# Transposes on 64x128 tiles, shorter runs for q and k, and a new order of steps in a fused attention and wave-MLP kernel

## The chip, the cores and the metric

The kernel runs on one core of a Trainium2 chip. The metric is the device time of one execution in microseconds; runs are compared by the median of several.

## What is computed

q, k and v have the shape (8, 8, 576, 64): batch, heads, positions, head dimension. Attention is local: each chunk of 64 positions sees only itself. Its output is rearranged to x of shape (8, 576, 512) and goes through a phase block with four weights.

```python
scores = (1 / sqrt(64)) * q_c @ k_c.T          # per batch, head and chunk of 64
attn = softmax(scores)
x = (attn @ v_c)                               # -> (8, 576, 512)
theta = x @ w_theta
zr, zi = x * cos(theta), x * sin(theta)
y = einsum('ts,bsd->btd', w_tok_r, zr) + einsum('ts,bsd->btd', w_tok_i, zi)
u = x + y
out = u + maximum(u @ w_ch, 0)
```

Inputs and output are float32; on the chip the matmuls work on float16.

## The kernel before

Four pairs of batches are worked through. A pair has 9 tiles of 128 rows, in five groups: A and B are two tiles each of the pair's first batch, C and D two tiles each of its second, M is the one tile in the middle that holds the last 64 positions of both. A step is one small stage of one group or tile, and its name in the table ORDER says which: `T.0M.1` is stage T of pair 0, group M, in PSUM slot 1.

The stages of a group: loads `q`, `k`, `v`; `T` transposes q and k on PE (`qk_t`), `tq` and `tk` copy the result out of PSUM; `S` the scores, `e` their exps; `V0`, `V1` attention times v for four heads each, `v0`, `v1` divide by the sums; `X` transposes x, `x` copies it; `H` is theta, `g` cosine and sine, `z` the products zr and zi. For group M the products of one half of the rows must change partitions, so `z` sends a tile `zmid` over SP's queue. Then tile by tile: `Y` (nine matmuls against the transposed token weights, for which all z of the batch and M must be there), `y` adds x, `U` and `u` transpose the sum, `W` multiplies by w_ch, `w` is the last addition and the store on SP's queue. Once per run: `lw.00` and `lw.01` load the token weights, `cw` casts the first, `TW` transposes them in three parts and `twd`, `twa` copy these out; `lt` and `lc` load the other two weights.

The steps of all engines are emitted in the order of the table, and each engine works through its own part of it strictly in that order. There are three two-bank PSUM slots (`wide`) for all stages up to H, and two one-bank slots (`thin`) for Y, U and W. q, k, v and most weights are loaded by POOL's queue, which casts them to float16; a load waits until its buffer is free (`nat`, eight of them for q and k; v has room for two pairs). Every 64x64 transpose is its own matmul with its own weight load, addressed to one quarter of the PE array. q and k lie in a tile with two successive positions per partition, so that a DMA reads 512 bytes in one piece.

Of the kernel before, what the change touches and what calls it, by code (L numbers as in the profile page):

```python
# [18 lines left out]
lw.00 q.0M init.00 cw.00 q.0B q.0A TW.00.0 v.0M k.0M q.0C k.0A new.00 T.0M.1 new.10  # L19
tq.0M k.0B tk.0M v.0A twd.00 S.0M.2 k.0C T.0A.1 twa.00 lt.00 e.0M V0.0M.0 q.0D T.0B.2  # L20
v.0B tq.0A tk.0A S.0A.1 tk.0B tq.0B V1.0M.2 v0.0M v.0C e.0A S.0B.0 V1.0A.1 v1.0M k.0D
v1.0A T.0C.2 V0.0A.1 e.0B tq.0C lw.01 tk.0C X.0M.0 q.1A S.0C.2 v0.0A q.1B x.0M X.0A.0
e.0C q.1M v.0D x.0A H.0M.1 H.0A.2 V1.0B.0 g.0M k.1A v1.0B g.0A V0.0B.1 v0.0B V0.0C.0
v0.0C k.1B V1.0C.1 k.1M v1.0C X.0B.2 T.0D.0 x.0B z.0A q.1C tq.0D tk.0D X.0C.1 x.0C z.0M
H.0B.2 q.2M S.0D.0 lc.00 g.0B v.1M TW.01.1 v.1A twd.01 q.1D TW.02.2 twa.01 twa.02 e.0D
H.0C.1 g.0C q.2B z.0B twd.02 Y.00.0 y.00 Y.02.1 U.00.0 V1.0D.2 T.1A.0 v1.0D u.00 tq.1A
V0.0D.1 tk.1A Y.01.0 v.1B v0.0D X.0D.2 T.1M.0 x.0D k.1D k.2B y.02 T.1B.1 y.01 tq.1M
U.02.1 U.01.0 k.1C k.2M z.0C tk.1B v.1D H.0D.2 u.02 tk.1M u.01 S.1A.0 W.01.1 w.01 g.0D
e.1A tq.1B W.02.0 Y.03.1 S.1B.2 V0.1A.1 S.1M.0 w.02 z.0D v0.1A e.1B q.2A e.1M Y.04.0
V1.1M.1 V0.1M.2 y.03 q.3A V1.1A.0 y.04 Y.06.1 v1.1A v1.1M v0.1M T.1D.0 y.06 tq.1D  # L30
# [6 lines left out]
x.1C w.04 e.2M tk.2B u.07 H.1C.2 tq.2B W.07.0 z.1D W.05.1 w.07 q.3D Y.11.0 v.2M w.05
U.10.1 new.20 V1.2M.0 g.1C u.10 S.2A.1 V0.2M.2 y.11 W.08.0 v.3C Y.12.1 e.2A z.1C k.2D
v0.2M w.08 v1.2M T.2C.2 S.2B.1 e.2B V1.2A.0 v1.2A v.2D Y.15.0 v.2C tk.2C V0.2A.0 tq.2C
y.12 y.15 T.2D.1 v.3A tq.2D v0.2A V1.2B.2 v1.2B Y.14.1 V0.2B.0 tk.2D X.2M.1 y.14 X.2A.2  # L40
U.15.0 x.2M Y.16.1 S.2D.1 x.2A v0.2B X.2B.0 k.3B y.16 S.2C.2 e.2C U.11.1 u.15 W.10.0
u.11 Y.18.1 w.10 x.2B e.2D y.18 H.2M.2 W.11.0 w.11 U.12.1 H.2A.0 g.2M z.2M V0.2D.1
V1.2C.2 U.18.0 u.12 W.15.1 u.18 w.15 W.12.0 v.3M w.12 v1.2C g.2A k.3C Y.17.1 V1.2D.0
k.3A v0.2D y.17 v1.2D T.3A.2 V0.2C.1 k.3M U.16.0 W.18.1 w.18 H.2B.0 u.16 tk.3A v0.2C
Y.13.0 g.2B U.17.1 tq.3A X.2C.1 y.13 u.17 v.3D T.3M.2 X.2D.0 x.2C U.14.0 W.16.1 u.14
tq.3M x.2D z.2A U.13.0 u.13 w.16 tk.3M H.2C.1 H.2D.0 g.2C W.13.0 W.14.1 T.3B.2 S.3M.1
g.2D z.2B w.13 S.3A.0 w.14 tq.3B tk.3B e.3M Y.20.0 Y.21.1 new.30 z.2C k.3D y.20 W.17.0
e.3A z.2D T.3D.2 V1.3A.1 w.17 tq.3D tk.3D v1.3A v.3B V1.3M.0 Y.24.0 T.3C.2 S.3B.1 v1.3M
tk.3C y.21 V0.3A.0 y.24 U.20.1 u.20 tq.3C Y.23.0 v0.3A X.3A.2 e.3B V0.3M.0 y.23 S.3C.1
U.21.1 e.3C W.20.0 u.21 Y.22.1 w.20 v0.3M x.3A y.22 U.24.0 H.3A.1 U.23.1 u.24 u.23  # L50
W.21.0 g.3A Y.28.1 V0.3C.2 V1.3B.0 w.21 v0.3C V0.3B.1 y.28 Y.27.0 W.23.1 v0.3B V1.3C.2
v1.3B y.27 S.3D.1 w.23 X.3M.0 x.3M e.3D v1.3C Y.25.0 y.25 U.27.1 u.27 H.3M.0 W.24.0 w.24
V1.3D.2 g.3M V0.3D.1 v1.3D W.27.1 v0.3D Y.26.0 w.27 z.3M U.22.1 y.26 X.3C.2 u.22 X.3D.0
X.3B.1 W.22.1 w.22 U.28.0 x.3B x.3D u.28 H.3B.1 U.25.1 z.3A u.25 W.28.0 W.25.1 g.3B
# [9 lines left out]
def kernel(  # L64
# [11 lines left out]
    nc = tc.nc  # L76
    B, H, S, D = q.shape
# [33 lines left out]
    nat = ctx.enter_context(tc.tile_pool(name="nat", bufs=8))  # L111
    tmp = ctx.enter_context(tc.tile_pool(name="tmp", bufs=3))
    pairp = ctx.enter_context(tc.tile_pool(name="pairp", bufs=2))
# [16 lines left out]
    wraw = pairp.tile([P, KT, S], FP32, name="wraw", tag="zi16")  # L130
# [16 lines left out]
    def load_qk(p, g, which):  # L147
        j0, bb, s0 = GROUPS[g]
        if (p, g) not in nats:
            nats[p, g] = nat.tile([P, 2, H, 2, D], FP16, name="qk16")  # L150
        t = nats[p, g][:, which]
        ap = (q, k)[which]
        if bb is None:
            for b in range(2):
                nc.gpsimd.dma_start(
                    t[half[b], :, 0, :],
                    ap[2 * p + b, :, s0 : s0 + CH, :].rearrange("h s d -> s h d"),
                )
            return
        nc.gpsimd.dma_start(  # L160
            t.rearrange("p h s d -> p h (s d)"),
            ap[2 * p + bb, :, s0 : s0 + GT, :].rearrange(
                "h (p s) d -> p h (s d)", s=2
            ),
        )

    nats = {}

    def load_v(p, g):
        j0, bb, s0 = GROUPS[g]  # L170
        slot = (p % 2) * NT + j0
        if bb is None:
            for b in range(2):
                nc.gpsimd.dma_start(
                    v16[half[b], slot, :, 0:D],
                    v[2 * p + b, :, s0 : s0 + CH, :].rearrange("h s d -> s h d"),
                )
            return
        for r in range(2):
            t0 = s0 + r * P  # L180
            nc.gpsimd.dma_start(  # L181
                v16[:, slot + r, :, 0:D],
                v[2 * p + bb, :, t0 : t0 + P, :].rearrange("h s d -> s h d"),
            )
# [19 lines left out]
    def tok_w(k3, slot):  # L204
        ps = psum2("ps_wT", slot, FP16)
        psv = ps.rearrange("p (r x) -> p r x", r=2)[:, :, 0 : 3 * (KT + 1) * CH]
        psv = psv.rearrange("p r (k t c) -> p r k t c", k=3, c=CH)
        for k in range(3):
            kt = 3 * k3 + k
            for tb in range(KT + 1):  # L210
                for r in range(2 if tb < KT else 1):
                    for h in range(2):
                        if kt < 2 * KT:
                            ri, jl = kt // KT, kt % KT
                            s0 = (jl // 2) * GT + (jl % 2) * CH + h * P
                        else:
                            ri, s0 = h, KT * P
                        nc.tensor.transpose(
                            psv[half[h], r, k, tb, :],
                            wnat[half[r], tb, ri, s0 : s0 + CH],  # L220
                            id16[half[r], half[r]],
                        )
        st["wT", k3] = psv

    def tok_w_copy(k3, r):
        psv = st["wT", k3]
        ks = slice(3 * k3, 3 * k3 + 3)
# [342 lines left out]
```

## Time and profile before

| | |
|---|---|
| median of 3 runs | 237.83 us (234.85 to 238.71) |
| the profiled execution | 235.57 us, its span 233.8 us |
| PE busy | 189.8 us, 81% of the span, 3834 matmuls |
| DVE, ACT, POOL busy | 125.9, 124.2, 76.3 us |
| DMA packets | 87939, of which 80608 under 512 bytes |

The span is what the trace covers; the time contains a little more around it. "Issue" in the chain of waits is time in which an engine waited for nothing that the profile shows. PEclk is the TensorE clock that was granted, as a share of 2.4 GHz. Bytes and packet sizes are those written, so a float32 run of 256 bytes in memory counts as 128.

### The profile page before, as it was taken

The numbers are of one execution on the slowest core, as the hardware profiler recorded it, in microseconds if no ns is written. First come the engines' busy times: TensorE is split into PE (matmuls) and PEld (weight loads), VectorE is DVE, ScalarE is ACT, GpSimd is POOL, SyncE is SP. The second block draws the span as 40 slices with busy tenths as digits, with TensorE's granted clock in tenths as the row PEclk, the third lists the DMA queues.
The fourth block names the chain that finished last, engine by engine and source line by source line (L and its number), as shares of the span: only waits on it lengthen the run. The fifth ranks groups of instructions, "written<-read, shape, count | busy, mean of one in ns | idle before, by whom it ended". The sixth has DMA issues, their size and how long they took to land.

```text
span 233.8 us, 8436 instructions
## 1 busy us (share of the span) xinstructions
PE 189.8 (81%) x3834; PEld 101.5 (43%) x3834; DVE 125.9 (54%) x248; ACT 124.2 (53%) x137; POOL 76.3 (33%) x98
## 2 busy tenths in 40 slices
PE   0252347959799899897949999999999999989971
PEld 0141323535445545453525445555554554444430
DVE  0032402843758784637554476878638784664351
ACT  2434266588572859987612946784763688020210
POOL 8895758877240651599600000000000000000000
PEclk9999999799999999999988999999999999999996
DMA  6999999999996799899991254232022354205444
GB/s 213 173 173 191 174 186 170 182 180 173 142 156 122 89 191 136 67 130 183 219 189 11 48 116 88 47 86 56 6 57 46 81 113 95 45 11 123 89 93 90
DMA packets 87939, 27.70 MB, mean 118 GB/s; under 512 B 80608, under 2 KB 82720, under 8 KB 87904
## 3 DMA queue, kind: packets, MB, share of 16 engines
q0 software_dynamic: 80896, 15.87, 80.2%
q1 hardware_dynamic: 7008, 11.29, 19.5%
q8 instruction: 30, 0.49, 0.9%
q14 instruction: 5, 0.04, 0.0%
HBM read 33.06 MB, written 9.44 MB: 182 GB/s over the span
## 4 chain that ended last, share of the span: by engine, by line
PE 70%; DVE 9%; issue 8%; DMA 6%; ACT 4%; POOL 1%; DVEq 0%; ACTq 0%; POOLq 0%
PE ps_y L441 30%; PE ps_theta L380 14%; PE ps_uw L477 11%; PE ps_qkT L249 4%; PE ps_uT L459 4%; DMA qk<-in_q_dram 3%; DMA qk<-in_k_dram 3%; PE ps_sT L289 3%; DVE u L450 2%; ACT kT L267 2%; DVE x L335 2%; PE ps_x L322 2%; PE ps_xT L355 2%; DVE qT L265 1%; DVE o L486 1%
## 5 line engine op out<-in xcount | busy, mean ns | idle before, releaser
L441 PEld LDWEIGHTS <-wT 128*128 128x128 f16 (+1 forms) x360 | 31.7, 103 | 38.2 <-issue 4.6
L441 PE MATMUL ps_y<-zi,wT 128*128 128x512 f16 (+1 forms) x180 | 45.4, 391 | 0.1
L441 PE MATMUL ps_y<-zr,wT 128*128 128x512 f16 (+1 forms) x180 | 42.3, 391 | 1.7 <-DVE o L486 1.7
L380 PE MATMUL ps_theta<-wtheta,xT 128*128 128x512 f16 x144 | 37.9, 411 | 1.7 <-ACT wT L234 1.2
L450 DVE TENSOR_TENSOR u<-ps_y,x 128x512 f16<-128x512 f32 x36 | 24.5, 688 | 25.0 <-PE ps_y L441 24.9
L477 PE MATMUL ps_uw<-wch,uT 128*128 128x512 f16 x144 | 35.9, 380 | 0.7 <-ACT uT L471 0.7
L486 DVE SCALAR_TENSOR_TENSOR o<-ps_uw,u 128x512 f32<-128x512 f32 x36 | 24.7, 688 | 20.6 <-PE ps_uw L477 20.6
L181 POOL DMA_DIRECT2D v<-in_v_dram x32 | 28.3, 903 | 8.1 <-PE ps_x L322 2.8
L471 ACT COPY uT<-ps_uT 128x512 f16<-128x512 f16 x20 | 11.8, 588 | 36.1 <-PE ps_uT L459 36.1
L265 DVE COPY qT<-ps_qkT 128x1024 f16<-128x1024 f16 (+1 forms) x20 | 12.7, 635 | 32.6 <-PE ps_qkT L249 20.3
L267 ACT COPY kT<-ps_qkT 128x1024 f16<-128x1024 f16 x16 | 16.2, 1015 | 25.0 <-DVE qT L265 20.8
L367 ACT COPY xT<-ps_xT 128x1024 f16<-128x1024 f16 (+1 forms) x20 | 18.3, 930 | 16.7 <-PE ps_xT L355 16.7
L335 DVE TENSOR_TENSOR x<-ps_x,recip 128x512 f16<-128x512 f32 (+1 forms) x40 | 25.5, 638 | 1.4
L249 PE MATMUL ps_qkT<-id,qk 64*64 64x64 f16 x1152 | 16.1, 203 | 11.8 <-issue 8.8
L396 ACT ACTIVATE cos<-ps_theta,pihalf 128x1024 f16<-128x1024 f32 (+1 forms) x20 | 20.6, 1030 | 6.9 <-PE ps_theta L380 6.7
L160 POOL DMA_DIRECT2D qk<-in_q_dram x16 | 14.2, 888 | 25.2 <-PE ps_x L322 9.5
L380 PEld LDWEIGHTS <-xT 128*128 128x128 f16 x144 | 14.3, 104 | 18.2 <-issue 5.3
L249 PEld LDWEIGHTS <-qk 64*64 64x64 f16 x1152 | 13.4, 114 | 14.9 <-issue 11.3
L302 ACT ACTIVATE eT<-ps_sT 128x1024 f16<-128x1024 f32 x16 | 16.4, 1026 | 6.5 <-PE ps_sT L289 6.4
L477 PEld LDWEIGHTS <-uT 128*128 128x128 f16 x144 | 12.9, 98 | 14.3 <-ACT uT L471 1.2
L400 ACT ACTIVATE sin<-ps_theta 128x1024 f16<-128x1024 f32 (+1 forms) x20 | 18.7, 935 | 0.0
L334 DVE RECIPROCAL recip<-ps_x 128x8 f32<-128x8 f32 (+1 forms) x40 | 7.8, 195 | 15.5 <-PE ps_x L322 15.0
(44 smaller groups left out, 184.1 us busy)
## 6 DMA issues: line engine op xcount, KB each, us to landing
out_dram<-o SPq DMA_DIRECT2D x72, 128.0 KB, 2.4
qk<-in_q_dram POOLq DMA_DIRECT2D x16, 256.0 KB, 6.8
qk<-in_k_dram POOLq DMA_DIRECT2D x16, 256.0 KB, 7.5
v<-in_v_dram POOLq DMA_DIRECT2D x32, 128.0 KB, 7.1
wraw<-in_moe_w_tok_r_dram SPq DMA_DIRECT2D x1, 1152.0 KB, 6.2
wnat<-in_moe_w_tok_i_dram POOLq DMA_DIRECT2D x1, 576.0 KB, 12.3
qk<-in_q_dram POOLq DMA_DIRECT2D x8, 64.0 KB, 7.0
v<-in_v_dram POOLq DMA_DIRECT2D x8, 64.0 KB, 6.5
```

The costliest lines, as they stand in the source:

```text
L181: nc.gpsimd.dma_start(v16[:, slot + r, :, 0:D], v[2 * p + bb, :, t0 : t0 + P, :].rearrange("h s d -> s h d"),)
L249: nc.tensor.transpose(psv[half[h], r, e, w, s, :], t[half[r], w, 2 * e + h, s, :], id16[half[r], half[r]],)
L267: nc.scalar.copy(out=t.rearrange("p x c t -> p x (c t)"), in_=ps.rearrange("p x s i -> p x i s"),)
L335: nc.vector.tensor_tensor(out=st[p]["x"][:, j0 : j0 + n, f * NE * D : (f + 1) * NE * D].rearrange("p c (h d) -> p c h d", h=NE), in0=psv[: ...
L367: nc.scalar.copy(out=xT[:, 0 : n * NDB].rearrange("p a (r c) -> p r a c", r=2), in_=psv)
L380: nc.tensor.matmul(ps[:, j * DM : j * DM + DM], xT[:, j * NDB + db, :], wtheta16[:, db, :], start=(db == 0), stop=(db == NDB - 1),)
L396: nc.scalar.activation(out=cos[:, 0:n].rearrange("p a e -> p (a e)"), in_=pin, func=AF.Sin, bias=pihalf, scale=1.0,)
L400: nc.scalar.activation(out=sin[:, 0:n].rearrange("p a e -> p (a e)"), in_=pin, func=AF.Sin)
L441: nc.tensor.matmul(ps[rows], wT[:, kt, cols], z[:, jz, :], start=(i == 0), stop=(i == 2 * KT),)
L450: nc.vector.tensor_tensor(out=u, in0=st[p].pop(("ps_y", j)), in1=st[p]["x"][:, j], op=ALU.add)
L477: nc.tensor.matmul(ps, uT[:, db * P : db * P + P], wch16[:, db, :], start=(db == 0), stop=(db == NDB - 1),)
L486: nc.vector.scalar_tensor_tensor(out=o, in0=st[p].pop(("ps_uw", j)), scalar=0.0, in1=u, op0=ALU.max, op1=ALU.add)
```

## The change

Transposes of q and k, of x and of the token weights use 128 columns of the array instead of 64, so that one instruction does what two did. q and k lie in their tile as v does, one position per partition and tile, with two heads next to each other; a group is loaded by two DMAs of 256-byte runs. The copies, scores and exps follow the new layout. `nat` has seven buffers, and `wraw` one of its own. The table ORDER is another one, with `lw.00` in it a second time near the end. Three of its lines, of 41 before and 41 after, and the core of the code:

```diff
-lw.00 q.0M init.00 cw.00 q.0B q.0A TW.00.0 v.0M k.0M q.0C k.0A new.00 T.0M.1 new.10
+lw.00 init.00 cw.00 q.0B TW.00.0 q.0A q.0M k.0B k.0A twd.00 T.0B.1 tk.0B lt.00 twa.00
...
+v0.3D lw.00 H.3A.1 u.20 w.23 g.3B U.21.0 u.21 g.3A W.20.1 w.20 Y.28.0 z.3B y.28 U.24.1
...
-    nat = ctx.enter_context(tc.tile_pool(name="nat", bufs=8))
+    nat = ctx.enter_context(tc.tile_pool(name="nat", bufs=7))
...
     def load_qk(p, g, which):
-        j0, bb, s0 = GROUPS[g]
         if (p, g) not in nats:
-            nats[p, g] = nat.tile([P, 2, H, 2, D], FP16, name="qk16")
-        t = nats[p, g][:, which]
-        ap = (q, k)[which]
...
-        nc.gpsimd.dma_start(
-            t.rearrange("p h s d -> p h (s d)"),
-            ap[2 * p + bb, :, s0 : s0 + GT, :].rearrange(
-                "h (p s) d -> p h (s d)", s=2
-            ),
-        )
-
-    nats = {}
+            nats[p, g] = nat.tile([P, 2, 2, H, D], FP16, name="qk16")
+        for rows, r, b, t0, n in parts(p, g):
+            nc.gpsimd.dma_start(
+                nats[p, g][rows, which, r],
+                (q, k)[which][b, :, t0 : t0 + n, :].rearrange("h s d -> s h d"),
+            )
...
     def qk_t(p, g, slot):
...
         for w in range(2):
             for e in range(NE):
-                for s in range(n):
+                for j in range(n):
                     for r in range(2):
-                        for h in range(2):
-                            nc.tensor.transpose(
-                                psv[half[h], r, e, w, s, :],
-                                t[half[r], w, 2 * e + h, s, :],
-                                id16[half[r], half[r]],
-                            )
...
+                        nc.tensor.transpose(
+                            psv[:, r, w, e, j, :],
+                            t[half[r], w, j, 2 * e : 2 * e + 2, :].rearrange(
+                                "s h d -> s (h d)"
+                            ),
+                            id16[half[r], half[r]],
+                        )
...
                 for r in range(2):
-                    for h in range(2):
-                        d0 = db * P + h * CH
-                        nc.tensor.transpose(
-                            psv[half[h], r, j * NDB + db, :],
-                            st[p]["x"][half[r], j0 + j, d0 : d0 + CH],
-                            id16[half[r], half[r]],
-                        )
+                    nc.tensor.transpose(
+                        psv[:, r, j * NDB + db, :],
+                        st[p]["x"][half[r], j0 + j, db * P : db * P + P],
+                        id16[half[r], half[r]],
+                    )
```

`parts` gives the two pieces of a group: two tiles of 128 rows of one batch, or for M 64 rows of each batch. The token weights' transposes change likewise: both halves of 64 rows go in one instruction.

Where the table moves instructions, at three places. POOL's queue at the start of the program, before and after (`qk_92`, `qk_103`, `qk_105` are pair 0's groups M, B, A before; `qk_100`, `qk_134`, `qk_137` its B, A, M after; `qk_166` is C before):

```order
L155 DMA qk_92<-in_q_dram 64x8x64 x2
masks.py:197 MEMSET id_79 128x128
masks.py:199 ISA
masks.py:199 AFFINE_SELECT id_79<-id_79 128x128
L160 DMA qk_103<-in_q_dram 128x8x128
L160 DMA qk_105<-in_q_dram 128x8x128
L174 DMA v_87<-in_v_dram 64x8x64 x2
L155 DMA qk_92<-in_k_dram 64x8x64 x2
L160 DMA qk_166<-in_q_dram 128x8x128
L160 DMA qk_105<-in_k_dram 128x8x128
L160 DMA qk_103<-in_k_dram 128x8x128
L181 DMA v_87<-in_v_dram 128x8x64 x2
```

```order
masks.py:197 MEMSET id_79 128x128
masks.py:199 ISA
masks.py:199 AFFINE_SELECT id_79<-id_79 128x128
L160 DMA qk_100<-in_q_dram 128x8x64 x2
L160 DMA qk_134<-in_q_dram 128x8x64 x2
L160 DMA qk_137<-in_q_dram 64x8x64 x2
L160 DMA qk_100<-in_k_dram 128x8x64 x2
L160 DMA qk_134<-in_k_dram 128x8x64 x2
L188 DMA wtheta_81<-in_moe_w_theta_dram 128x4x512
L160 DMA qk_137<-in_k_dram 64x8x64 x2
L168 DMA v_87<-in_v_dram 128x8x64 x2
L168 DMA v_87<-in_v_dram 64x8x64 x2
```

M's loads stand behind those of B and A, C's have left the start, and each load of 128 rows of q or k is now two.

ACT's queue from its first copies to the first cosine, before and after:

```order
L234 COPY wT<-ps_wT 128x3x2x128
L298 ACTIVATE eT<-ps_sT 128x2x256
L267 COPY kT<-ps_qkT 128x1024 x2
L302 ACTIVATE eT<-ps_sT 128x1024 x2
L267 COPY kT<-ps_qkT 128x1024
L367 COPY xT<-ps_xT 128x2x4x64
L302 ACTIVATE eT<-ps_sT 128x1024
L367 COPY xT<-ps_xT 128x2x8x64
L396 ACT_TABLE_LOAD
L396 ACTIVATE cos_718<-ps_theta,pihalf 128x512
```

```order
L263 COPY kT<-ps_qkT 128x1024
L227 COPY wT<-ps_wT 128x3x256
L263 COPY kT<-ps_qkT 128x1024
L289 ACTIVATE eT<-ps_sT 128x1024 x2
L289 ACTIVATE eT<-ps_sT 128x2x256
L352 COPY xT<-ps_xT 128x2x4x64
L352 COPY xT<-ps_xT 128x2x8x64
L381 ACT_TABLE_LOAD
L381 ACTIVATE cos_508<-ps_theta,pihalf 128x512
```

The third k copy and the third full exp, both of group C, no longer stand ahead of the first cosine.

PE around the first Y, before and after; the first `ps_y` is PE's instruction 1,694 before and 942 after, of 7,670 and 5,798 in all:

```order
L380 LDWEIGHTS xT
L380 MATMUL ps_theta<-wtheta_81,xT 128x512
L380 LDWEIGHTS xT
L380 MATMUL ps_theta<-wtheta_81,xT 128x512
L441 LDWEIGHTS wT
L441 MATMUL ps_y<-zr_170,wT 128x512
```

```order
L245 LDWEIGHTS qk_327
L245 MATMUL ps_qkT<-id_79,qk_327 128x64
L245 LDWEIGHTS qk_327
L245 MATMUL ps_qkT<-id_79,qk_327 128x64
L426 LDWEIGHTS wT
L426 MATMUL ps_y<-zr_322,wT 128x512
```

Before, theta of C is the last step ahead of the first Y; after, it is the transposition of pair 1's group M, and theta of C comes later.

## Rows read from the trace of the kernel before

**Rows 1.** Page, part 1: busy time of the engines, share, instructions.

```profile
PE 189.8 (81%) x3834; PEld 101.5 (43%) x3834; DVE 125.9 (54%) x248; ACT 124.2 (53%) x137; POOL 76.3 (33%) x98
```

**Rows 2.** Windows: stretch, length, busy time per engine, granted clock, DMA share, GB/s.

```profile
17.00:52.20 35.20, 20.02 (x641) 11.91 (x642) 13.62 (x31) 19.50 (x21) 24.74 (x32) 0.95 1.88 180
52.20:117.20 65.00, 59.66 (x1420) 32.39 (x1418) 40.23 (x81) 46.95 (x51) 36.20 (x44) 1.00 1.48 147
117.20:124.50 7.30, 4.26 (x81) 1.91 (x66) 3.63 (x8) 1.01 (x1) 0.22 (x1) 0.77 1.67 150
124.50:233.80 109.30, 101.56 (x1510) 51.83 (x1508) 66.12 (x122) 51.40 (x60) 0.00 (x0) 0.98 0.31 69
```

**Rows 3.** Chain that ended last, in order of time: start, length, what.

```profile
10.17 6.81 DMA qk<-in_k_dram
...
17.50 2.93 issue
...
24.48 2.80 issue
...
30.88 2.31 issue
...
33.52 5.24 PE ps_theta L380 x12
...
52.33 3.88 PE ps_y L441 x18
...
59.66 1.67 issue
...
117.37 3.04 issue
```

**Rows 4.** Windows of PE between stalls: matmuls (x), clock, DMA share, GB/s.

```profile
17.45:24.45 7.00, 2.55 (x128) 1.00 1.74 185
24.45:30.85 6.40, 2.20 (x131) 1.00 1.78 185
30.85:46.85 16.00, 11.91 (x258) 0.89 1.90 176
46.85:59.60 12.75, 10.34 (x258) 1.00 2.05 175
```

**Rows 5.** Page, part 3: the queue that brings instructions; packets, MB, share.

```profile
q8 instruction: 30, 0.49, 0.9%
```

**Rows 6.** Windows in which only q and k arrive, and only v.

```profile
12.50:15.00 2.50, 1.33 (x64) 1.01 (x62) 1.39 (x4) 0.39 (x1) 2.50 (x4) 1.00 1.82 181
35.00:36.50 1.50, 1.50 (x5) 0.54 (x4) 0.00 (x0) 1.49 (x3) 1.33 (x2) 1.00 2.40 155
```

**Rows 7.** Timeline of POOL: two issues of 128 rows, two of 64.

```profile
3.25 1.78 POOL L160 DMA_DIRECT2D qk<-in_q_dram  x2
...
27.20 1.37 POOL L155 DMA_DIRECT2D qk<-in_q_dram  x2 [0.79 <-DMA v<-in_v_dram]
```

**Rows 8.** DMA issues until 17 us, and from 35 to 60: KB, us to landing.

```profile
qk<-in_k_dram POOLq DMA_DIRECT2D x3, 256.0 KB, 6.8
...
zr<-zmid SPq DMA_DIRECT2D x1, 64.0 KB, 6.7
```

**Rows 9.** Groups of instructions by shape: busy us, mean ns of one, idle before.

```profile
L302 ACT ACTIVATE eT<-ps_sT 128x1024 f16<-128x1024 f32 x16 | 16.4, 1026 | 6.5 <-PE ps_sT L289 6.4
...
L367 ACT COPY xT<-ps_xT 128x512 f16<-128x512 f16 x4 | 2.4, 592 | 7.4 <-PE ps_xT L355 7.4
...
L396 ACT ACT_TABLE_LOAD x8 | 10.3, 1283 | 0.5 <-PE ps_theta L380 0.4
...
L335 DVE TENSOR_TENSOR x<-ps_x,recip 128x512 f16<-128x512 f32 x32 | 22.1, 692 | 1.1
```

**Rows 10.** Chain in order of time again: transposes of q and k, and of u.

```profile
56.69 0.55 PE ps_qkT L249 x64
...
125.37 0.33 PE ps_uT L459 x4
```

More of the change, by code (lines that the diff above doesn't have):

```diff
@@ L37 @@
[L37 to L42, printed above, removed]
@@ L223, in tok_w @@
-        st["wT", k3] = psv
+                rows = slice(0, P if tb < KT else CH)
+                if tb < KT:
+                    at = k * KT * P + (tb // 2) * GT + (tb % 2) * CH
+                    to = ps[:, at : at + GT].rearrange("p (c r x) -> p c r x", c=2, r=2)
+                    to = to[:, :, 0]
+                else:
+                    at = 3 * KT * P + k * CH
+                    to = ps[:, at : at + CH]
+                for h in range(2):
+                    if kt < 2 * KT:
+                        ri, jl = kt // KT, kt % KT
+                        s0 = (jl // 2) * GT + (jl % 2) * CH + h * P
+                    else:
+                        ri, s0 = h, KT * P
+                    nc.tensor.transpose(
+                        to[half[h]],
+                        wnat[rows, tb, ri, s0 : s0 + CH],
+                        id16[rows, rows],
+                    )
@@ L238, in qk_t @@
+        eng = nc.scalar.copy if r else nc.vector.tensor_copy
+        eng(out=wT[:, ks, c], in_=most[:, :, c])
+        if r == 0:
+            eng(
+                out=wT[:, ks, KT * P : S],
+                in_=ps[:, 3 * KT * P : 3 * S].rearrange("p (k c) -> p k c", k=3),
+            )
     def qk_t(p, g, slot):
[L239 to L240 removed]
+        n = 1 if g == "M" else 2
         ps = psum2("ps_qkT", slot, FP16)
[L242 removed]
+        psv = ps.rearrange("p (r w e j c) -> p r w e j c", r=2, w=2, e=NE, j=2)
@@ L261, in qk_copy @@
         name = "qk"[which] + "T"
[L262 removed]
+        t = tmp.tile([P, 2, NE, n, CH], FP16, name=name, tag=f"{name}{n}", bufs=n + 1)
         st[p][name, g] = t
[L264 to L270 removed]
+        copy = nc.scalar.copy if which and n == 2 else nc.vector.tensor_copy
+        if n == 2:
+            flat = "p r e j c -> p r (e j c)"
+            copy(out=t.rearrange(flat), in_=ps.rearrange(flat))
+        else:
+            copy(out=t[:, :, :, 0], in_=ps[:, :, :, 0])
     def scores(p, g, slot):
[L273 to L274 removed]
+        n = 1 if g == "M" else 2
         qT, kT = st[p].pop(("qT", g)), st[p].pop(("kT", g))
         ps = psum2("ps_sT", slot)
[L277 to L278 removed]
+        psv = ps.rearrange("p (h j e c) -> p h j e c", h=2, j=2, e=NE)
+        for j in range(n):
             for e in range(NE):
                 for h in range(2):
[L281 to L289 removed]
+                    for r in range(2):
+                        nc.tensor.matmul(
+                            psv[half[r], h, j, e, :],
+                            kT[half[h], r, e, j, :],
+                            qT[half[h], r, e, j, :],
+                        )
         st[p]["ps_sT", g] = ps
@@ L352, in x_t @@
                 for r in range(2):
-                    for h in range(2):
-                        d0 = db * P + h * CH
-                        nc.tensor.transpose(
-                            psv[half[h], r, j * NDB + db, :],
-                            st[p]["x"][half[r], j0 + j, d0 : d0 + CH],
-                            id16[half[r], half[r]],
-                        )
+                    nc.tensor.transpose(
+                        psv[:, r, j * NDB + db, :],
+                        st[p]["x"][half[r], j0 + j, db * P : db * P + P],
+                        id16[half[r], half[r]],
+                    )
         st[p]["ps_xT", g] = psv
```

179 lines of the change are left out of this document (68 added, 111 removed).

## The prediction

> **What bounds the kernel now.** I read four views, from the coarse to the fine. First the totals: PE is busy 189.8 of 233.8 us and no other engine is above 55% [rows 1]. That is an average over unlike stages, so next the windows: PE is busy 20.0 of the 35.2 us from 17 to 52.2; then 59.7 of 65, 4.3 of 7.3 and 101.6 of the last 109.3 [rows 2]. From 52.2 us on PE is the bound, with some 16 us of idle time in all (5.3 + 3.0 + 7.7). Before that it mostly waits, and the chain of waits says for what: the second q/k landing at 17.0 us, then stretches called "issue", 2.93, 2.80 and 2.31 us, after them slow theta matmuls, and at 52.33 the first Y [rows 3]. Y is the largest block of PE work (36 steps of 1.94 us), and everything before the first Y serves to make it possible.
>
> "Issue" means that nothing in the trace was waited for, yet the stalls cut the transposes in the middle. Counting PE's matmuls between stalls settles what they are: 128 and 131 between the first three, 258 from the third to one at 46.87 and 258 from there to the one at 59.66 [rows 3, 4], all close to multiples of 128. A matmul comes with its weight load, so 128 matmuls are 256 instructions; queue 8 moved 30 packets, 0.49 MB [rows 5], about 16 KB each, and the 7,670 PE instructions of the program divided by 30 are 256. So PE's program arrives in blocks of 256 instructions, and while the DMA engines are full a block comes late. At 8.6 ns per transpose (64 in 0.55 us, [rows 10]) a block of transposes lasts little over a microsecond; the two shortest spacings of stalls are 7.0 and 6.4 us.
>
> The Trainium skill (Runtime: NRT & Kernel Launch, section Instruction fetch mechanics) has the same 16 KiB blocks of 256 instructions, but says that crossing a boundary is mostly hidden. By that the change would gain nothing from fewer instructions. The trace disagrees here: 2.9 us at one boundary.
>
> **The change, part by part.** *Loads.* A q or k group was one DMA with 512-byte runs (128 rows, two positions each); now it is two DMAs with 256-byte runs, as v has always been. A stretch in which q and k alone arrive moves 181 GB/s, one of v alone 155 [rows 6]. So 262 KB took 1.44 us and now takes 2 x 0.85 = 1.69 us. POOL pays 0.89 us per issue of 128 rows and 0.70 of 64 [rows 7], hence 1.78 us per group, which is a little slower than the data; this is the new price, +0.34 us for each of 32 loads, 10.9 us over the run. It is hidden as long as loads run ahead of PE; where they don't, see below.
>
> The Trainium skill (DMA: Bandwidth & Descriptors, section Specifications) asks for transfers of at least 512 bytes for full rate and so speaks against this edit. The trace agrees that shorter is slower, at 181 against 155 GB/s; by the page alone the loads would cost more than that, which it doesn't price for this size.
>
> *Time of the first Y, before: 52.3.* Worked out for the new order from its rows: the identity costs POOL 0.54 us first (masks), so the loads start at about 1.8. q.0B, q.0A, q.0M, k.0B, k.0A are eight issues of 0.89 and two of 0.70: 10.3 us, and with 6.8 us to land [rows 8] k.0A is there at 17.0, as the second k is now. theta's weights and k.0M, v.0A, v.0M, v.0B follow until 17.5 and land until 24.5, each before its use. From 17 us ACT's queue is the chain. Its full-size steps take 1.03 and those of M 0.6: the k copies end at about 18.0 and 19.0, three exps at 21.7. Then PE and DVE make x of group M (two V steps, two normalisations and a transposition, of which the longest piece is a full normalisation of 0.69; I allow 2.4, to 24.1). ACT copies xT of M and of A (25.7), loads its table, 1.28 (27.0), and does cos and sin of M (28.3) [rows 9]. DVE multiplies two half tiles (0.8, by the same 0.69 for a full one), SP sends zmid, which took 6.7 us to land while loads were running [rows 8]: 36 us. I add 1 us for the hops and 1 us for one late block: the second boundary comes after some 5 us, near 22. **First Y at 38, 14.3 us earlier.** Beside this PE has theta of M, A and B (20 matmuls of 0.43, 8.6 us cold) and the transposes, so it isn't the limit. Less is done by then: before, theta of C (8 x 0.216 = 1.7) and C's X and V steps came ahead of the first Y, now only T.1M instead; 3.0 us of PE work is still owed. Net **-11.3**.
>
> *Fewer instructions.* 936 of 3,834 matmuls go, with their weight loads. For the first stretch this is inside the 38 us: PE reaches the first Y after 941 instructions instead of 1,693, two to three boundaries instead of five. Later, the stalls at 59.66 (1.67) and 117.37 (3.04) [rows 3] have no reason to stay: **-4.7**. With the second goes the dip behind it: from 117.2 to 124.5 the granted clock averaged 0.77 [rows 2], that is the lower of its two levels (1.2 and 2.4 GHz) for 3.4 of the 7.3 us, which costs half of them: **-1.7**.
>
> *The transposes' own time.* Four 64x64 transposes run side by side now (64 in 0.55 us, though 64 columns each); a 64x128 one takes two quarters of the array, so two run side by side, with half as many. I take no gain and no loss, as the same columns pass. Bounds: at the same 8.6 ns each, 32 take 0.28 us; that is -0.27 for the equivalent of 13 full T steps after the first Y and, X having half as many, -0.14 for 15 X steps, -5.6; one after another, by the 128-wide u transposes (4 in 0.33, half for 64 columns: 41 ns each, 32 in 1.3 us), +0.75 and +0.38: +15 [rows 10].
>
> *New load waits.* After the first Y PE has 15.6 us of work before it needs k.1D (4 Y, 7.8; 16 theta and W matmuls, 3.5; 3 u transposes, 1.0; small steps, 3.4): at 53.6. By then 34 full loads at 0.85, 14 half ones at 0.42 and 1.7 MB of weights at 181 GB/s (9.4) must have passed: 44 us, from about 7 on (the token load on SP, 1.3 MB, comes first, at the same 181 GB/s), plus an estimated 2 to land: 53. That is no reserve. v.1D is 22 issues (some 19 us) later and needed 22 us later, with hardly any. I take **+5** (0 to 10).
>
> *Clock.* Theta ran at 437 ns per matmul at 33.5, after a start in which PE mostly waited, Y at 216 from 52.33 [rows 3]: 512 columns at 1.2 and at 2.4 GHz. The granted clock's own 0.95 for 17 to 52.2 [rows 2] doesn't tell the two apart. The first Ys now come after short steps and may start at the lower level: two of them would cost 3.9. I take **+2** (0 to 4).
>
> At nothing: the rearranged copies and exps, same elements per instruction; nat with 7 buffers instead of 8, which POOL reaches only when it is far ahead; and the repeated token load on SP near the end, 1.3 MB behind zmid's transfer and ahead of the stores of 14 row tiles; the DMA engines are mostly idle there, and if the four output buffers didn't cover it, about 5 us once.
>
> **Sum.** -11.3 - 4.7 - 1.7 + 5 + 2 = -10.7. The profiled execution took 235.57 (span 233.8), so 224.9; the median of the runs shown is 237.83, 1.0096 times that, so **227**.
>
> **The rivals.** *Larger gain (0.17).* The loads keep up, the clock is there and the transposes reach their lower bound: 5 + 2 + 5.6 less, 212.3, times 1.0096 is 214; so 214 to 221. For it: v already arrives at the new rate. Against it: no reserve at k.1D.
>
> *The stalls aren't the program's (0.15).* If "issue" returns at other places, or a block is late whatever PE does (the DMA queue stays full longer), 4.7 + 1.7 and some 3 us of the start come back: 224.9 + 9.4 = 234.3, times 1.0096 is 236.5, no measurable change. Against it: the multiples of 128.
>
> *128 columns don't run side by side (0.08).* +15 by the bound: 239.9, times 1.0096 is 242, about the edge to slower.
>
> *Loads become the bound (0.10): the slower case.* If packets and not bytes limit, a 128-row DMA costs what the one with twice the bytes did, 1.44 us. k.1D then lands at 7 + 49 + 10 + 9.4 + 2 = 77 instead of 53, PE waits 24 us where I allow 5: 224.9 + 19, times 1.0096, is about 246. It decides at k.1D: with 34 loads ahead, +0.31 us per load (1.16 us, 113 GB/s) eats the whole gain. Against it: 155 GB/s in a v stretch, with that very packet. For it: such a stretch is short, and POOL's own 0.89 us per issue lies just above the 0.85 that the data take.
>
> **How the numbers follow.** The forecast, with its own bounds 221 to 233, has 0.50. Two per cent is about what runs from 234.85 to 238.71 can tell, so "faster" is below 233.1: the forecast nearly whole and the larger gain, 0.66. "Same" up to 242.6 takes the stalls' case, its edge and half of the columns' case: 0.22; slower 0.12. The range 217 to 237 leaves out the bottom of the second case and the last two.
>
> **What would show it.** The first Y near 38 us in the chain, no "issue" over 2 us later than 60, about 23 packets in queue 8, q and k landing at about 155 GB/s, T at 0.5 to 0.6 us for 32. It is wrong if the first Y is after 45, if PE waits for k or v by more than 10 us in all, or if T takes over 0.8 us.

## The result, and the profile after

The changed kernel takes 220.28 us (median of 4 runs, 218.63 to 222.0) against 237.6 for the kernel before on the same chip: 0.929 of its time, 95% interval 0.919 to 0.939. That is 17.3 us less where the forecast was 10.7 less. The profiled execution took 218.63, its span is 216.8 us, 17.0 less than before. A run more than 1.5% above the fastest of its kernel counts as slow, and here and below the medians take in all runs, the ratios only the others.

The totals and the queue that brings instructions, from the page after (they answer to [rows 1] and [rows 5]):

```profile
PE 189.2 (87%) x2898; PEld 101.0 (47%) x2898; DVE 126.6 (58%) x248; ACT 119.0 (55%) x133; POOL 104.3 (48%) x130
...
q8 instruction: 22, 0.36, 0.7%
```

PE's busy time has hardly moved, though 936 matmuls are gone; 22 packets instead of 30 brought its program. What went is idle time, and the waits of PE say which. Before (engine, line, what was waited for: us in total, times, longest; the five lines that end in issue):

```profile
PE ps_qkT L249 <- issue: 8.8, 3, 3.0
PE ps_xT L355 <- issue: 4.0, 2, 2.3
...
PE ps_wT L218 <- issue: 1.2, 1, 1.2
...
PE ps_theta L380 <- issue: 0.5, 1, 0.5
...
PE ps_sT L289 <- issue: 0.3, 1, 0.3
```

After, the head of the same view:

```profile
PE ps_wT L211 <- ACT wnat L184: 9.0, 1, 9.0
PE ps_y L426 <- DMA zr<-zmid: 3.4, 1, 3.4
PE ps_qkT L245 <- DMA qk<-in_k_dram: 2.0, 3, 0.8
PE ps_x L309 <- DMA v<-in_v_dram: 1.8, 2, 1.4
```

Before, PE waited 14.8 us for "issue" in eight places; after, no line of the view names it. All other waits together went from 23.7 to 22.5, PE's busy time from 189.8 to 189.2. So -14.8 - 1.2 - 0.6 = -16.6 of the -17.0: the change is worth what the stalls called "issue" cost, and nearly nothing else.

The chain of waits after, in order of time (it answers to [rows 3] and [rows 10]):

```profile
12.62 2.40 POOL v L168 x3
15.03 7.59 DMA v<-in_v_dram
...
27.96 3.35 PE ps_theta L365 x8
...
31.65 1.47 PE ps_wT L211 x30
33.12 1.85 PE ps_theta L365 x8
...
36.11 0.92 ACT sin L385
...
37.59 0.83 ACT wT L227
...
38.87 2.05 PE ps_y L426 x9
...
60.35 0.57 PE ps_qkT L245 x32
...
86.89 7.50 DMA zr<-zmid
94.43 4.06 PE ps_y L426 x18
...
141.04 0.55 issue
```

The first Y runs at 38.87, at 228 ns per matmul; theta ahead of it already runs at 231 ns. A full T step of 32 transposes takes 0.57 us. The longest "issue" behind 40 us is 0.55. One new wait stands out: the transfer of zmid, 7.50 us long, in front of the first Y of pair 1's first batch. The windows (as [rows 2]) show the same from outside:

```profile
17.00:38.90 21.90, 17.03 (x345) 10.01 (x346) 12.09 (x28) 12.81 (x15) 19.00 (x24) 1.00 2.18 162
38.90:90.50 51.60, 51.09 (x928) 27.28 (x929) 36.27 (x74) 37.79 (x42) 48.80 (x58) 1.00 2.22 180
90.50:94.50 4.00, 0.64 (x27) 0.48 (x20) 1.20 (x3) 3.15 (x4) 2.62 (x3) 1.00 2.02 202
```

PE is busy 51.09 of 51.60 us behind the first Y, at a granted clock of 1.00 (2.4 GHz); the hole at 90.5 is the wait for zmid.

### The profile page after: what moved, and what is told of

Read it like the earlier page. It is cut to its first block, busy times and chain, and to the rows that moved or that the text cites. A ratio compares the mean times of both kernels' runs of the same rounds, so it can differ in the third digit from the quotient of the medians.

```text
span 216.8 us, 6577 instructions
## 1 busy us (share of the span) xinstructions
PE 189.2 (87%) x2898; PEld 101.0 (47%) x2898; DVE 126.6 (58%) x248; ACT 119.0 (55%) x133; POOL 104.3 (48%) x130
## 4 chain that ended last, share of the span: by engine, by line
PE 70%; ACT 8%; DMA 7%; POOL 6%; DVE 5%; issue 1%; POOLq 0%; ACTq 0%
PE ps_y L426 30%; PE ps_uw L462 13%; PE ps_theta L365 13%; POOL qk L160 5%; PE ps_uT L444 4%; DMA v<-in_v_dram 4%; DMA zr<-zmid 3%; PE ps_x L309 3%; PE ps_xT L340 2%; PE ps_qkT L245 2%; PE ps_sT L276 2%; ACT cos L381 2%; DVE x L322 2%; ACT sin L385 2%; ACT kT L263 1%
## 5 line engine op out<-in xcount | busy, mean ns | idle before, releaser
L426 PE MATMUL ps_y<-zr,wT 128*128 128x512 f16 (+1 forms) x180 | 41.4, 380 | 3.4 <-DMA zr<-zmid 3.4
L426 PE MATMUL ps_y<-zi,wT 128*128 128x512 f16 (+1 forms) x180 | 44.3, 380 | 0.0
L365 PE MATMUL ps_theta<-wtheta,xT 128*128 128x512 f16 x144 | 36.3, 399 | 0.3 <-ACT xT L352 0.3
L168 POOL DMA_DIRECT2D v<-in_v_dram x40 | 34.1, 876 | 4.7 <-DMA v<-in_v_dram 1.5
L160 POOL DMA_DIRECT2D qk<-in_k_dram x40 | 34.1, 886 | 3.3 <-DMA qk<-in_k_dram 0.8
L160 POOL DMA_DIRECT2D qk<-in_q_dram x40 | 34.3, 885 | 1.7 <-issue 0.6
L381 ACT ACTIVATE cos<-ps_theta,pihalf 128x1024 f16<-128x1024 f32 (+1 forms) x20 | 20.6, 1031 | 10.3 <-PE ps_theta L365 5.8
L289 ACT ACTIVATE eT<-ps_sT 128x1024 f16<-128x1024 f32 (+1 forms) x20 | 18.4, 939 | 4.2 <-PE ps_sT L276 4.0
L245 PE MATMUL ps_qkT<-id,qk 64*128 64x64 f16 x576 | 13.1, 197 | 2.8 <-DMA qk<-in_k_dram 2.0
L444 PE MATMUL ps_uT<-id,u 128*128 128x128 f16 x144 | 14.0, 220 | 1.1 <-DVE u L435 1.0
L263 DVE COPY qT<-ps_qkT 128x1024 f16<-128x1024 f16 x16 | 10.8, 686 | 5.4 <-ACT kT L263 4.7
```

The lines of the kernel that those rows point to most:

```text
L160: nc.gpsimd.dma_start(nats[p, g][rows, which, r], (q, k)[which][b, :, t0 : t0 + n, :].rearrange("h s d -> s h d"),)
L168: nc.gpsimd.dma_start(v16[rows, slot + r, :, 0:D], v[b, :, t0 : t0 + n, :].rearrange("h s d -> s h d"),)
L263: copy(out=t.rearrange(flat), in_=ps.rearrange(flat))
L365: nc.tensor.matmul(ps[:, j * DM : j * DM + DM], xT[:, j * NDB + db, :], wtheta16[:, db, :], start=(db == 0), stop=(db == NDB - 1),)
L381: nc.scalar.activation(out=cos[:, 0:n].rearrange("p a e -> p (a e)"), in_=pin, func=AF.Sin, bias=pihalf, scale=1.0,)
L426: nc.tensor.matmul(ps[rows], wT[:, kt, cols], z[:, jz, :], start=(i == 0), stop=(i == 2 * KT),)
```

## The experiments

Ten kernels ran. For every one the same account can be drawn from two views, the totals and the waits of PE: span = PE busy + "issue" + other waits + about 5 us that the view gives to nobody. The last four columns are of the profiled execution, which can lie some 2 us to either side of the median.

| kernel | median us | ratio to before (95%) | span | PE busy | issue | other waits |
|---|---|---|---|---|---|---|
| before | 237.6 | | 233.8 | 189.8 | 14.8 | 23.7 |
| after | 220.28 | 0.929 (0.919 to 0.939) | 216.8 | 189.2 | 0 | 22.5 |
| e1_order_only | 240.88 | 1.008 (1.004 to 1.011) | 236.8 | 191.5 | 19.2 | 20.6 |
| e2_code_only | 221.06 | 0.932 (0.928 to 0.936) | 218.9 | 188.9 | 0 | 24.5 |
| e3_quarters_TX | 230.59 | 0.973 (0.968 to 0.978) | 230.8 | 194.6 | 9.9 | 21.5 |
| e4_no_reload | 219.6 | 0.924 (0.917 to 0.931) | 218.8 | 190.9 | 0 | 22.6 |
| e5_loads_8 | 224.27 | 0.943 (0.937 to 0.950) | 222.5 | 192.2 | 0 | 25.1 |
| e5_loads_16 | 228.2 | 0.963 (0.957 to 0.970) | 226.8 | 193.3 | 0 | 28.4 |
| e6_zmid_early | 216.15 | 0.912 (0.908 to 0.916) | 214.3 | 188.8 | 0 | 20.3 |
| e7_zmid_lt | 217.0 | 0.915 (0.910 to 0.920) | 214.6 | 189.3 | 0 | 20.1 |
| e8_dup_early | 241.36 | 1.017 (1.010 to 1.024) | 240.6 | 201.0 | 10.0 | 24.7 |
| e9_dup_late | 233.84 | 0.988 (0.981 to 0.995) | 232.7 | 200.5 | 4.2 | 22.7 |

e1, e2, e4 and both e5 leave out the second token load, whose data nothing reads. In e2 and both e5 `wraw` also shares a buffer with one of the `zi` tiles again, as in the kernel before.

### Order alone, code alone

The two halves of the change apart. e1 is the kernel before with the new table; e2 is the changed code with the old table and eight `nat` buffers.

```diff
 # e1_order_only, against before
-lw.00 q.0M init.00 cw.00 q.0B q.0A TW.00.0 v.0M k.0M q.0C k.0A new.00 T.0M.1 new.10
+lw.00 init.00 cw.00 q.0B TW.00.0 q.0A q.0M k.0B k.0A twd.00 T.0B.1 tk.0B lt.00 twa.00
...
 # e2_code_only, against after
-lw.00 init.00 cw.00 q.0B TW.00.0 q.0A q.0M k.0B k.0A twd.00 T.0B.1 tk.0B lt.00 twa.00
+lw.00 q.0M init.00 cw.00 q.0B q.0A TW.00.0 v.0M k.0M q.0C k.0A new.00 T.0M.1 new.10
```

> The kernel before with the new order alone (without the second token load): 64x64 transposes, 512-byte runs, eight q/k buffers stay. The first Y is PE instruction 1,484 then, against 940 in the changed kernel. Theory A, the order is worth what it is only with fewer instructions: late blocks of PE's program come back as stretches of issue of 2 to 3 us in the transposes, three to four of them ahead of the first Y, which falls at 44 to 48 us; in all 226 to 233 us. Rival B, the order alone did it: first Y at 39 to 41, in all 219 to 223. Rival C, q and k in 512-byte runs cost nothing extra here and load faster, so that it beats the changed kernel: under 218.

> The changed code (64x128 transposes, 256-byte runs) in the order of before, with eight q/k buffers. The first Y is PE instruction 1,148, against 1,692. Theory A: the stretches of issue of over 2 us go (9.3 us ahead of the first Y, 4.7 behind it), but the order keeps C's loads, copies and theta ahead of the first Y, and the longer loads take some of it back: first Y at 44 to 49, in all 226 to 232 us. Rival B, the order is all: no change against before, 235 to 240. Rival D, fewer instructions are all: 218 to 222.

e1 measured 240.88, above the ranges of A, B and C; e2 221.06, in the range of rival D and within the changed kernel's own interval, where A had 226 to 232. So the new code (instructions, layout and loads together) is worth the gain as far as the intervals can tell, and the new table without it none. Why the table gives nothing shows in the chain of e1:

```profile
34.86 1.38 issue
...
37.50 4.39 issue
...
42.21 3.96 PE ps_y L441 x9
...
62.12 3.25 issue
```

The first Y is indeed early, at 42.21 against 52.33 [rows 3], but the stalls are still there. One of 4.39 us stands directly ahead of that Y, and the Y then runs at 440 ns per matmul, twice as long as at the full clock; another stall follows at 62.12. By the account the table saves 3.1 us of other waits (23.7 to 20.6) and pays 4.4 us of "issue" and 1.7 us of PE time at a lower clock. In e2 the first Y comes later, at 43.6, as the timeline of PE shows:

```profile
43.59 1.24 PE L426 MATMUL ps_y<-zr,wT 128*128 128x512 f16 x5
```

and yet the time is that of the changed kernel within what the intervals can tell. Its other waits are 2.0 us longer (24.5 against 22.5) and its span 2.1. So when the first Y runs is no measure of the end: what counts is PE's idle time in all.

### The instructions put back

The changed kernel with q, k and x transposed in 64x64 quarters again; loads, layout and table as in the change.

```diff
-                        nc.tensor.transpose(
-                            psv[:, r, w, e, j, :],
-                            t[half[r], w, j, 2 * e : 2 * e + 2, :].rearrange(
...
+                        for h in range(2):
+                            nc.tensor.transpose(
+                                psv[half[h], r, w, e, j, :],
+                                t[half[r], w, j, 2 * e + h, :],
+                                id16[half[r], half[r]],
+                            )
```

> The changed kernel with q, k and x transposed as 64x64 again (864 more matmuls with their weight loads), everything else as changed: loads, layout, order. It prices the instructions alone. Theory A: the transposes' own time is the same (0.55 us for a q/k group), but blocks of the program come late again, stretches of issue of 1 to 3 us appear in the chain: +5 to +10 us, 225 to 230. Rival B: under +2 us, 220 to 222. If a 64x128 transpose is quicker in the array, the 18 groups' worth of T would show it: up to +5 without any issue.

230.59 us, 10.3 more than the changed kernel for 864 matmuls, just over the upper end of what was expected. The chain of e3 shows where:

```profile
38.92 2.05 PE ps_y L427 x9
...
41.47 1.62 PE ps_y L427 x7
43.09 2.91 issue
46.00 3.86 PE ps_y L427 x11
...
70.78 5.68 PE ps_y L427 x18
...
105.94 6.98 PE ps_y L427 x18
```

The first Y is in time, at 38.92. Then a block is late in the middle of a Y, and the eleven matmuls behind the stall take 351 ns each instead of 231. By the account: 9.9 us of "issue", 5.4 us more PE time, 1.0 less of other waits: 14.3, where the spans of the two profiled executions lie 14.0 apart (this one was the slowest of its kernel, the changed kernel's the fastest). The 5.4 is lower clock in the main (the mean granted clock is 0.964, against 0.996), but only some 3.0 of it stands behind these stalls: 1.3 for the eleven matmuls at 46.00 and 1.7 for the eighteen at 70.78, behind a stall of 3.06 us, which took 3.99 in the changed kernel. Another 2.9 stands at 105.94, behind the wait for zmid, where the changed kernel's profiled execution took 4.06 us for the same eighteen.

So 10.3 of the 17.3 us come back with the instructions. e3 is not e1, though: 29 and 30 packets of program, nearly the same table, and yet 9.9 and 19.2 us of "issue". What differs between them (loads, layout, copies, the token weights' transposes, and with these the places where the blocks end) was not taken apart.

### What a block costs, and where

Does a block come late only while the DMA engines are full? Two steps X are issued 17 times instead of once, into the same place, in pair 0 (about 47 and 65 us, loads running) or in pair 3 (176 and 189 us, the loads of q, k and v over): 512 matmuls, 1,024 instructions, four blocks more, and q8 moves 26 packets instead of 22 in both.

```diff
+        for again in range(17 if (p, g) in ((0, "C"), (0, "D")) else 1):   # e8; e9: (3, "C"), (3, "D")
-        for j in range(n):
+            for j in range(n):
...
```

> The changed kernel with the transposes of x of pair 0's groups C and D issued 17 times each instead of once, into the same place: 512 matmuls and their weight loads more, 1,024 instructions or four blocks, at about 48 and 54 us, where the DMA share is 2.2. In the changed kernel 16 such transposes take 0.34 us and 32 take 0.57, so 512 are 7.4 to 10.9 us of PE work on the path. Theory (a block comes late while the DMA engines are full, and PE's clock falls behind it): four blocks in some 10 us, at the 2.3 to 3.0 us that a late block cost before, give 8 to 13 us more than the work: 236 to 243 us, with stalls called issue inside these steps. Rival (instructions cost their own time and nothing else, wherever they stand): 227 to 231, equal to the run with the same transposes late.

> The changed kernel with the transposes of x of pair 3's groups C and D issued 17 times each instead of once: the same 512 matmuls and four blocks more, but between 164 and 179 us, where loads are over and the DMA share is about 0.3. The work is the same 7.4 to 10.9 us. Theory (blocks are late only while the DMA engines are full): 227 to 231 us, no stall called issue over 1 us, and 8 or more below the run with the same transposes early. Rival (a block costs its 2 to 3 us wherever instructions run that fast): 236 to 243, within 2 us of the early run.

Early 241.36, as the theory had it; late 233.84, between the two, with stalls over 1 us that the theory did not allow. The chains of e8 and of e9:

```profile
50.73 2.04 PE ps_xT L341 x128
52.77 3.60 issue
...
67.90 2.90 issue
70.81 1.94 PE ps_xT L341 x121
...
72.85 1.41 issue
```

```profile
178.18 2.69 issue
180.86 3.43 PE ps_xT L341 x128
184.29 0.30 issue
```

Exactly 128 matmuls stand between two stalls again, here with nothing but one kind of transpose. From PE's start on one block to its start on the next, in the windows of PE (length, busy, clock, DMA share, GB/s), two of e8:

```profile
50.70:56.35 5.65, 2.04 (x128) 0.94 2.21 175
70.80:74.25 3.45, 2.04 (x128) 1.00 0.02 5
```

Two of e9, the first ahead of its stall at 178.18, the second behind it; and SP's issue of the second token load in e9:

```profile
176.10:178.20 2.10, 2.08 (x139) 1.00 1.02 335
180.85:184.55 3.70, 3.43 (x128) 0.54 0.02 4
```

```profile
171.75 0.53 SPq L177 DMA_DIRECT2D wraw<-in_moe_w_tok_r_dram  x1
```

e9 is thus quiet only in part: the second token load is issued at 171.75, and 335 GB/s are moving directly ahead of the stall of 2.69 us, so that this stall shows nothing about idle DMA engines. The stretches at a DMA share of 0.02 do.

So a block needs 3.45 and 3.70 us with the DMA engines all but idle, 5.65 us at a DMA share of 2.21, and 6.85 and 5.91 us in the kernel before (from the end of one stall to the end of the next, 20.43 to 27.28 to 33.19 [rows 3]; the 7.0 and 6.4 of [rows 4] run from the start of one stall to the start of the next). PE runs through 128 of these transposes in 2.04 us at the full clock and is stopped either way, for 1.41 us in the quiet stretch of e8; loads make the stop longer. The work itself is 4 x 2.04 = 8.2 us. Against the changed kernel's 220.3 the late repetition cost 13.6, so 5.4 beyond the work, the early one 21.1, so 12.9. Stalls are 4.2 and 10.0 us of this; the wait for zmid, 3.3 us in e9 and 4.8 in e8, is another 1.5 of the difference. "Only while the DMA engines are full" falls by the 1.41 us; "it costs its 2 to 3 us anywhere alike" falls as well, since the first three stalls of e8 are 2.05 to 3.60 us long. What remains: a stall is the block's time less what PE finds to do with 256 instructions.

The Trainium skill (Runtime: NRT & Kernel Launch, section Instruction fetch mechanics) says that the engine fetches its next page while executing the current one, and that this is hidden because an engine works off instructions more slowly than the fetch fills them. The first half agrees with the runs here (by the trace's records of queue 8 the next packet starts at 71.93 in e8, 1.12 us into the 128 matmuls that begin at 70.81); the second does not, for matmuls as short as these: 2.04 us of work against 3.45 us at the least.

### The loads' reserve, and the second token load

e4 takes `lw.00` near the end away. The e5 pair adds to it loads of 128 rows of q that nobody reads, behind each q load of pair 1's groups A to D, three of which stand ahead of k.1D.

```diff
 # e4 and e5
-v0.3D lw.00 H.3A.1 u.20 w.23 g.3B U.21.0 u.21 g.3A W.20.1 w.20 Y.28.0 z.3B y.28 U.24.1
+v0.3D H.3A.1 u.20 w.23 g.3B U.21.0 u.21 g.3A W.20.1 w.20 Y.28.0 z.3B y.28 U.24.1
...
 # e5: range(1) in e5_loads_8, range(2) in e5_loads_16
+        if p == 1 and which == 0 and g != "M":
+            for _ in range(1):
+                more = scr.tile([P, H, D], FP16, name="more")
+                nc.gpsimd.dma_start(more, q[b, :, t0 : t0 + n, :].rearrange("h s d -> s h d"))
```

> The changed kernel without the second token load on SP near the end, whose data nothing reads. By the prediction it costs nothing: within 0.5 us. If the stores behind it held up the last output buffers, it is up to 5 us faster.

> The changed kernel (without the second token load) with 8 more loads of 128 rows on POOL's queue, two behind each q load of pair 1's groups A to D, into a buffer that nothing reads. Six of them stand ahead of k.1D: 5.3 us of POOL and 5.1 us of data. It measures the reserve of the loads. Theory no reserve (the prediction's): T.1D waits about 5 us for k.1D and the whole takes 5 to 7 us more, 225 to 228. Theory reserve of several us: under +2, 220 to 222.

> As the run with 8 more loads, with 16 (four behind each q load of pair 1's groups): 10.7 us of POOL ahead of k.1D, 14 in all. No reserve: +11 to +14, 231 to 235. A reserve of 3 us or more at k.1D: +5 to +9; hidden entirely: under +2.

Without the second token load 219.6 us: it costs nothing that can be measured. For the e5 pair the expectations count twice the loads that the kernels carry: the line stands behind the loop over a group's two pieces, so there is one (or two) per group, 4 and 8 in all. The pages say so: POOL x134 and x138, against x130. Their POOL time, 4 x 0.88 = 3.5 and 8 x 0.88 = 7.0 us, compares with +4.7 and +8.6 us measured against e4. By the account PE's other waits are 2.5 and 5.8 us longer than in e4 and its busy time 1.3 and 2.4: all but some 1.0 to 1.2 us of the added POOL time comes back as waits, and some lower clock on top. The waits of PE in e5_loads_16:

```profile
PE ps_qkT L252 <- DMA qk<-in_k_dram: 5.5, 5, 2.7
PE ps_x L316 <- DMA v<-in_v_dram: 4.5, 7, 1.4
```

10.0 us for k and v instead of 3.8. POOL issues k.1D (`47.09` on its timeline after, `52.73` in e5_loads_16, six added loads later):

```profile
47.09 1.81 POOL L160 DMA_DIRECT2D qk<-in_k_dram  x2
```

```profile
52.73 1.84 POOL L161 DMA_DIRECT2D qk<-in_k_dram  x2
```

and the chain of e5_loads_16 has T waiting for exactly this landing at 60.4. In the changed kernel the second of the two issues, at 48.0, lands by the median of 6.2 us at about 54.2 (an estimate), and T.1A and directly behind it T.1D run from 54.3 on. The load is there just in time: hardly any reserve, and no wait.

### The wait for zmid taken away

The wait at 86.89 is the largest that the change brought, and it came with the table: e1 has it too (3.2 us on PE), e2 has not. e6 emits z.1M, which sends zmid, 27 steps earlier, behind w.08; e7 also moves theta's weights behind v.0M in POOL's queue, for an earlier first Y.

```diff
-k.2C w.08 v.2B H.1B.0 v.3M u.04 U.07.1 u.07 x.1A new.20 W.06.0 w.06 k.2B v.3C W.04.1
+k.2C w.08 z.1M v.2B H.1B.0 v.3M u.04 U.07.1 u.07 x.1A new.20 W.06.0 w.06 k.2B v.3C W.04.1
...
 # e7 beside it
-T.0A.2 tq.0B tk.0A tq.0A S.0B.1 k.0M v.0A v.0M v.0B e.0B S.0A.0 e.0A T.0M.2 tq.0M tk.0M
+T.0A.2 tq.0B tk.0A tq.0A S.0B.1 k.0M v.0A v.0M lt.00 v.0B e.0B S.0A.0 e.0A T.0M.2 tq.0M tk.0M
```

> The changed kernel with one step moved: pair 1's products of group M (z.1M, which sends zmid over SP) stand right behind w.08 on DVE instead of behind H.1D, some 5 us earlier; cosine and sine of M are ready at 74.2 us. In the changed kernel the first Y of pair 1's first batch waits 3.4 us for zmid's transfer, 91.0 to 94.4. Theory: that wait goes, -2.5 to -3.5 us, 217 to 218, and nothing takes its place. Rival: another wait ends there (cosine of B or C at 90.7, DVE's u copies a little later): under -1.

> As the one with z.1M earlier, and theta's weights loaded behind v.0M instead of ahead of k.0M. In the changed kernel v.0M lands at 22.6 us and PE waits for v; 512 KB of theta's weights (0.75 us of POOL, 2.9 us of data at 181 GB/s) stand ahead of it. Theory: v.0A and v.0M land 1 to 3 us earlier, the first Y comes 1 to 2 us earlier, in all 215.5 to 217. Rival: theta of M now waits for its weights, or ACT's queue ends there anyway: no further gain.

e6 takes 216.15 us, about 4 us less than the changed kernel, a little more than was expected, and 9% less than the kernel before: the lowest median of all. The line for zmid is gone from PE's waits, and its chain runs through the place on PE:

```profile
85.79 5.30 PE ps_theta L364 x24
...
91.99 3.99 PE ps_y L425 x18
```

The spans lie 2.5 us apart. The rest fits the clock, though it is argued and not shown: behind the wait the changed kernel's profiled execution took 4.06 us for eighteen Y matmuls, e4, the same program up to there, 5.74 at a granted clock of 0.71:

```profile
94.54 5.74 PE ps_y L426 x18
```

So the wait cost 3.2 to 3.4 us, and in some executions 1.7 more.

e7 adds nothing (217.0): its first Y is at 37.87, e6's at 37.95.

## Why the prediction was right or wrong

227 was forecast and 220.28 measured, within 217 to 237 but 7 us below the forecast.

**What bounds the kernel.** Right. The stalls called "issue" are PE's program arriving in blocks: 22 packets where about 23 were forecast, no stall behind 60 us longer than 0.55, and putting the instructions back brings the stalls back (e3). The cause given for the lateness, full DMA engines, is part of it: e8 shows a block 1.41 us late at a DMA share of 0.02.

**Time of the first Y, -11.3.** This step failed in its reason, though its figure held (38 forecast, 38.87 measured), which is in part luck. The path was another one. Forecast were k.0A's landing at 17, ACT's copies and exps, zmid's landing at 36 and 2 us for hops and a late block. In the chain after, the start is POOL's issues up to 15.0, then v's landing at 22.6; theta, held to be off the path, follows, at first at 419 ns per matmul, and at the end ACT's cosine, sine and last copy of the token weights, until 38.42. zmid was sent at 29.80 and 30.35 and, at 5.6 and 5.7 us to land, there by about 36.1. The gain, -11.3, was derived from the new order. But the order without fewer instructions gives nothing (e1), and the new code without the order gives the whole gain as far as the intervals tell (e2), with a first Y at 43.6. The step had let the saved boundaries go by as part of the 38 us ("two to three boundaries instead of five"), and charged the rest to the order. The account puts it right: 14.8 us of "issue" in all is what the new code took away, not the 4.7 of the two later stalls; the order is worth at most 2 to 3 us of other waits, and the medians of e2 and the changed kernel, 0.8 apart, don't tell that from nothing. That the three terms together, -11.3 - 4.7 - 1.7 = -17.7, come near the -17.0 of the spans is luck of the same kind.

**Fewer instructions, -4.7 and -1.7.** Both came: no stall at 59.66 or 117.37, and the granted clock is 1.00 from 17 to 212 us. In e3 the price of the clock behind such stalls is seen again, some 3.0 us.

**The transposes' own time, nothing.** Right for q and k: 32 in 0.57 us where 64 took 0.55. Neither bound was near, and the rival of columns that don't run side by side is out. Left out were the token weights' transposes, which got dearer: 30 in 1.47 us, where the chain before has 49 in 0.66 at 48.10. That is one reason why PE's busy time fell by only 0.6 us in all.

**The loads.** The rate came as forecast, by the stretch from 92.5 to 100 us in the windows after, in which only q, k and v were being loaded:

```profile
92.50:100.00 7.50, 5.57 (x114) 3.25 (x116) 3.37 (x6) 2.55 (x4) 5.34 (x8) 1.00 2.36 160
```

160 GB/s, with the stores of out among them. POOL is busy 104.3 instead of 76.3 us; its issues are on the chain at the start, up to 15.0 us, and, as e5 shows, nearly so at k.1D.

**New load waits, +5.** Mis-sized: 0. "No reserve" was nearly right, as e5 shows by 8.6 us for eight loads, and the place, k.1D, too. But a load that comes just in time is no wait. PE waits 3.8 us for k and v in all (2.5 for k before), every one of them ahead of 23 us.

**Clock, +2.** Mis-sized: 0. Theta at 33.12 already runs at 231 ns, where the eight at 27.96 still took 419 each. (The granted clock doesn't tell the two apart: it is 1.00 for 25.7 to 31.3 as well.) PE was busy 13.7 of the 14.9 us from 24.0 to 38.9, with no stall for a block; where there is one, as in e1, the first Y is slow (440 ns). These two terms are the 7 us by which the forecast was too high: -10.7 - 7 = -17.7.

**At nothing: the second token load and seven `nat` buffers.** e4 confirms the first; e2, which has eight buffers, is no faster. Not named in the prediction was the wait for the second zmid, 3.4 us on PE.

**The rivals.** The time lies in the band of the larger gain (214 to 221), for two of its three reasons: the loads keep up and the clock is there; the transposes did not get faster. The stalls' return, the columns and the loads as the bound did not happen; the last needs only a few loads more, as e5 shows.

**What stays open.** Why a block takes 5.65 to 6.85 us under load and 3.45 to 3.70 without is open in part. The trace's records of queue 8 narrow it down. In the kernel before, PE resumes at 20.42, 27.27 and 33.20, each time 1.4 to 1.5 us after a packet of that queue has landed (19.00, 25.80, 31.83), one more sign that these stalls are the program's. The transfer of the packet itself takes 0.94 and 0.94 us before the second and third of these and 0.96 and 1.16 in the quiet stretches of e8 and e9. What differs is its start: 4.44 and 3.62 us after PE has resumed in the kernel before and 3.24 in e8 under load (only 1.06, though, behind 61.33 in the kernel before), 1.12 in both quiet stretches. So the time is lost ahead of the transfer and not in it; what the packet waits for there was not taken apart. Open is also why e1 has twice the stalls of e3 with nearly as many instructions.

## What to carry to other kernels

Where a profile shows "issue" on PE inside rows of small matmuls, count the matmuls between two such stalls; if it is 128 each time, the program is the bound there, and an instruction saved is worth more than its own time. Draw up the engine's idle time by cause over the whole span before costing a change by the date of one event: the first Y moved by 10 us in e1 and the end did not. And look for what has no reserve without adding a wait for it: just in time costs nothing until something else is put in front.

## What the runs showed of the hardware

- A block of 256 PE instructions took 3.45 to 3.70 us to arrive with the DMA engines idle and 5.65 to 6.85 us with loads running (e8, e9, the kernel before); 128 transposes of 64 rows took 2.04 us, and PE stopped for 1.41 us even in a quiet stretch of e8.
- Behind such a stop the granted clock can fall: 0.54 in the stretch from 180.85 to 184.55 of e9, where 128 transposes took 3.43 us instead of 2.04. In e3 this cost some 3.0 us beside 9.9 us of stalls. Not every stop shows it: behind the one of 2.90 us in e8 the clock is 1.00 from 70.80 to 74.25.
- The Trainium skill (DMA: Bandwidth & Descriptors, section Specifications) asks for 512 bytes and more per transfer. The shorter runs of q and k are slower, 160 against 181 GB/s [rows 6], and cost this kernel little: PE waits 3.8 us for k and v in all, 2.5 before.
